# Linear-attention output: r times the state from zero-padded 64-row halves of the array, instead of block-diagonal copies on 128 rows

## The chip, the cores and the metric

The kernel runs on one core of a Trainium2 chip. The metric is device time in microseconds (us) of one execution, start to end; the median of several runs is compared. TensorE (PE in the profile) multiplies, VectorE (DVE) and ScalarE (ACT) work elementwise, GpSimd (POOL) does little here, SyncE (SP) issues the transfers.

## What is computed

The first half is a recurrent linear attention (RWKV-5) for 4 batches, 8 heads, 768 steps and a head width of 48; the second half is a feed-forward network over all 3072 tokens.

```python
state = zeros(B, H, D, D)
for t in range(S):
    cur = (u * k_t)  outer  v_t                 # per head
    y[:, :, t] = r_t @ (state + cur)            # per head, D x D
    state = w[:, :, None] * state + k_t outer v_t
x = y as (3072 tokens, 8 * 48 = 384 features)
out = ((x @ w1) * (x @ w2) @ w3) @ w_out         # 384 -> 1024 -> 1024 -> 384
```

## The kernel before

**Units.** The time steps are cut into 6 chunks `c` of 128 steps, and each chunk is taken for the 4 batches `b` in turn: 24 units `n`. A chunk is two halves `a` of 64 steps. Heads are held in pairs: array `X[rows(i), p]` has head `2p+i` on 64 partitions, `i` = 0 (even) or 1 (odd), of which 48 are used.

**Steps of a unit.** `scale` multiplies k and r by powers of w (L310). `diagonal` makes the u-term (L319 to L321) and eight diagonal blocks of the table `AT` (L326, ScalarE). `turn`, or in later units `turn_blocks`, `turn_places` and `turn_rows`, transposes k and r to features on partitions (L342, or L352, L362 and L367). `pairs` multiplies k with v for the change of the state (L389) and k with r for the table (L395), updates the state twice, once for each half (L403, L408, L409, VectorE), and merges the table into `AT` (L416, VectorE). `output` makes y transposed, features on partitions: r times the state (L473), then the table times v (L483) accumulated onto it, and copies the sum to `xT` (L488, ScalarE).

**The state on the array.** The state `st[b]` holds pair `p` as 48 columns for 128 partitions, even head above, odd head below. L473 multiplies all 128 rows at once, so its stationary operand must be block-diagonal: `spread` (L420, ScalarE) copies the two heads of each pair into different columns of `wide`, whose other columns stay zero. It does so once for the state at the chunk's start (`spread(0, n)`, not in chunk 0) and once for the state after the first half (`spread(1, n)`), two instructions each time, 44 calls and 88 instructions in all. L473 then takes 32 of the 96 columns of a pair at a time: a tile of 128 rows and 32 columns of the array, twelve matmuls for each half. L483, L389 and L395 use tiles of 64 rows and 64 columns; the feed-forward matmuls and the transposes use the whole array.

**PSUM.** `ps_y` is one tile of two banks, one bank for each half `a`, with one buffer. The two banks of `psF` serve all feed-forward products in turn: L500 (x times w1), copied out by ScalarE (L502); L505 (x times w2), multiplied with that copy by VectorE (L506).

**Order.** The feed-forward work on chunk `c-1` and the preparation of its weights stand beside the units of chunk `c` (the lists `beside`): conversion of the weights from 64 to 32 bits (L266 to L272, ScalarE and VectorE), w3 folded with w_out (L296 to L301), then the products `o` (L539 to L553). The engines' queues are in order; a scheduler of the framework decides the order in which each engine's instructions stand, and a few of them are interleaved. In the trace a 32-bit matmul is two pairs of instructions, a weight load (PEld) and a matmul (PE).

Of the kernel before, what the change touches and what calls it, by code (L numbers as in the profile page):

```python
# [8 lines left out]
F32 = mybir.dt.float32  # L9
# [12 lines left out]
def kernel(  # L22
# [10 lines left out]
    moe_w_out: bass.AP,  # L33
    out: bass.AP,
):

# [18 lines left out]
    nc = tc.nc  # L57
    B, H, S, D = r.shape
    P = 128
    C = 128  # L60
    T = C // 2
    HT = T // 2
    NCH = S // C
    PAD = 64
    NP = H // 2
    DM = H * D
    DF = moe_w3.shape[0]
    KM = DM // P
# [7 lines left out]
    Q = 32  # L76
    PD = 2 * D

    const = ctx.enter_context(tc.tile_pool(name="const", bufs=1))

    def rows(i):
        return slice(i * PAD, (i + 1) * PAD)
# [21 lines left out]
    raws = [const.tile([P, RAW], U64, name=f"raw{i}") for i in range(NRAW)]  # L104


    st = [const.tile([P, NP, D], F32, name=f"st{b}") for b in range(B)]
    wide = [[const.tile([P, NP, PD], F32, name=f"wide{a}{i}") for i in range(2)] for a in range(2)]
    two = const.tile([P, 1], F32)
    nc.vector.memset(two, 2.0)  # L110
    wucol = const.tile([P, NP, 1], F32)
# [5 lines left out]
        nc.gpsimd.memset(t[:, :, D:PD], 0.0)  # L117
    for t in krs:
        nc.gpsimd.memset(t[:, :, :, D:PAD], 0.0)
    for t in wide[1] + wide[0]:  # L120
        nc.gpsimd.memset(t, 0.0)
    for t in tts:
        nc.gpsimd.memset(t[:, :, :NP], 0.0)

# [1 line left out]
    units = [(c, b) for c in range(NCH) for b in range(B)]  # L126
# [35 lines left out]
    for i in range(2):  # L162
# [4 lines left out]
                      in_=u.rearrange("h d -> (h d)").rearrange("(o n) -> o n", o=1).to_broadcast([P, DM]))  # L167
# [15 lines left out]
    with tc.tile_pool(name="once", bufs=1) as once, tc.tile_pool(name="psW", bufs=2, space=PSUM) as psW:  # L183
# [12 lines left out]
        for l in range(LEVELS):  # L196
            n = 1 << l
# [6 lines left out]
        for g in range(2):  # L204
            nc.vector.tensor_copy(out=both[:, g, :, T:], in_=both[:, g, :, :T])
            ps = psW.tile([P, NP, C], F32, tag="w", name=f"ps_p{g}")
# [11 lines left out]
    def body(arm, fast):  # L218
# [7 lines left out]
        psY = arm.enter_context(tc.tile_pool(name="psY", bufs=1, space=PSUM))  # L226
# [5 lines left out]
        else:  # L232
# [6 lines left out]
            for l in range(LEVELS):  # L239
                n = 1 << l  # L240
                by = wn[:, l].to_broadcast([P, NP, n])
# [6 lines left out]
            ps = psT.tile([P, NP, C], F32, tag="t", name="ps_pr")  # L248
# [55 lines left out]
        kT, rT, AT, xT = {}, {}, {}, {}  # L304
# [65 lines left out]
        def pairs(n):  # L370

            c, b = units[n]
            kk = krs[n % NS][:, 0]
            if fast:
                au = psA.tile([C, 2, 512], F32, tag="a", name=f"ps_a{n}")
                ps = au[:, :, :NP * T].rearrange("s i (p t) -> s i p t", p=NP)
            else:
                for l in range(LEVELS):
                    level(n, l)
                kk = work.tile([C, H, PAD], F32, tag="rl", bufs=1, name=f"kk{n}")  # L380
                nc.gpsimd.tensor_mul(kk, krs[n % NS][:, 0], pn[:, 0])
                au = psA.tile([C, 2, 512], F32, tag="a", name=f"ps_u{n}")

            up = au[:, :, NP * T:NP * (T + D)].rearrange("x a (p e) -> x a p e", p=NP)
            last = c == NCH - 1
            for p in range(NP):
                for i in range(2):
                    for a in range(1 if last else 2):
                        nc.tensor.matmul(up[rows(i), a, p, :], lhsT=kk[rows(a), 2 * p + i, :],  # L389
                                         rhs=vnat[n % NV][rows(a), 2 * p + i, 0:D], start=True, stop=True)  # L390
            if fast:
                for p in range(NP):
                    for a in range(2):
                        for i in range(2):
                            nc.tensor.matmul(ps[rows(a), i, p, :], lhsT=kT[n][rows(i), p, rows(a)],  # L395
                                             rhs=rT[n][rows(i), p, 2 * a:2 * a + 2], start=True, stop=True)
            by = wc.to_broadcast([P, NP, D])
            if c:
                spread(0, n)
            for a in range(1 if last else 2):  # L400
                if not c and not a:
                    if fast:
                        nc.vector.tensor_mul(st[b], up[:, a], by)  # L403
                    else:
                        nc.vector.tensor_copy(out=st[b], in_=up[:, a])
                elif fast:

                    nc.vector.tensor_add(st[b], up[:, a], st[b])  # L408
                    nc.vector.tensor_mul(st[b], st[b], by)  # L409
                else:  # L410
                    nc.vector.tensor_mul(st[b], st[b], by)
                    nc.vector.tensor_add(st[b], up[:, a], st[b])
                if not a:
                    spread(1, n)
            if fast:
                nc.vector.copy_predicated(AT[n], later.bitcast(I32)[:, None, None, :].to_broadcast([C, 2, NP, T]), ps)  # L416

        def spread(a, n):
            for i in range(2):
                nc.scalar.copy(out=wide[a][n % 2][rows(i), :, i * D:(i + 1) * D], in_=st[units[n][1]][rows(i)])  # L420

        def level(n, l):
            L = 1 << l
# [31 lines left out]
        def output(n):  # L455
            c, b = units[n]
            rw = rT[n]
            if not fast:
                rw = work.tile([P, NP, C], F32, tag="kl", bufs=1, name=f"rw{n}")
                for p in range(NP):  # L460
                    nc.gpsimd.tensor_mul(rw[:, p].rearrange("x (a t) -> x a t", a=2),
                                         rT[n][:, p].rearrange("x (a t) -> x a t", a=2),
                                         pw[:, p, None, :].to_broadcast([P, 2, T]))
            yt = psY.tile([P, 2, 512], F32, tag="y", name=f"ps_y{n}")
            ps = yt[:, :, :KM * T].rearrange("x a (q t) -> x a q t", q=KM)


            blocks = [(p, j, divmod(3 * p + j, P // Q)) for p in range(NP) for j in range(3)]
            to = lambda a, q, g: ps[g * Q:(g + 1) * Q, a, q, :]
            held = range(0 if c else 1, 2)  # L470
            for a in held:
                for p, j, (q, g) in blocks:
                    nc.tensor.matmul(to(a, q, g), lhsT=wide[a][n % 2][:, p, j * Q:(j + 1) * Q], rhs=rw[:, p, 2 * a:2 * a + 2] if fast else rw[:, p, rows(a)],  # L473
                                     start=(q == 0), stop=False, skip_group_check=True)

            vv = vnat[n % NV].rearrange("t h d -> t (h d)")
            parts = [(h, f) for h in range(H) for f in range(h * D // PAD, ((h + 1) * D - 1) // PAD + 1)]
            seen = set()
            for h, f in sorted(parts, key=lambda e: (e[0] * D > e[1] * PAD, e[1])):
                x = h * PD + f * PAD - h * D  # L480
                q, g = divmod(f, 2)
                for a in range(2):
                    nc.tensor.matmul(ps[rows(g), a, q, :], lhsT=vv[rows(a), x:x + PAD], rhs=AT[n][rows(a), h % 2, h // 2, :],  # L483
                                     start=(a not in held and (a, g) not in seen), stop=True, skip_group_check=True)
                    seen.add((a, g))
            if b == 0:
                xT[c] = work.tile([P, KM, NT], F32, tag="xT", bufs=2, name=f"xT{c}")
            nc.scalar.copy(out=xT[c][:, :, b * C:(b + 1) * C].rearrange("x q (a t) -> x a q t", a=2), in_=ps)  # L488


        abt, lead = {}, 3 if fast else 1
# [110 lines left out]
        diagonal(0)  # L602
        turn(0)
        pairs(0)
        asked = 2
        for c in range(NCH):
# [4 lines left out]
            for b in range(B):  # L611
                n = c * B + b
                while asked <= (n + 3 if n + 3 >= free else n + 2):
                    load(asked, "kr")
                    asked += 1
                load(n + 2, "v")
                if n + 1 < min(NU, free):
                    scale(n + 1)
                if n + 1 < NU:
                    diagonal(n + 1)  # L620
                    if n + 1 >= free:
                        turn_rows(n + 1)
                if n + 1 < min(NU, free):
                    turn(n + 1)
                if free <= n + 2 < NU:
                    scale(n + 2)
                    turn_blocks(n + 2)
                for step in plan[2 * b]:
                    step()
                output(n)  # L630
                if free <= n + 2 < NU:
                    turn_places(n + 2)
                if n + 1 < NU:
                    pairs(n + 1)
                for step in plan[2 * b + 1]:
                    step()
# [41 lines left out]
```

## Time and profile before

| what | value |
|---|---|
| median of 6 runs | 526.64 us (525.91 to 528.13) |
| the profiled execution | 526.08 us, of which the profile's span is 524.1 us |
| PE busy | 496.1 us, 95% of the span |
| PE weight loads busy | 324.8 us, 62% |
| DVE busy | 281.4 us, 54% |
| ACT busy | 195.4 us, 37% |
| L473, r times the state | 1056 matmul instructions, 25.2 us busy |
| L483, the table times v | 1152 matmul instructions, 24.4 us busy |
| L420, copies of the state | 88 instructions, 30.7 us of ACT |
| L488, y out of PSUM | 24 instructions, 11.4 us of ACT |

A row of a group gives the time in which any of its instructions ran and the mean time of one; matmuls overlap, so the sum of the single times is much larger than the busy time. The share of an engine is a mean over stages: up to about 50 us VectorE and ScalarE are the busy ones, after that PE is busy almost throughout.

### The profile page before, as it was taken

How to read it: one execution, taken by the hardware profiler on the slowest of the kernel's cores; microseconds unless marked ns; L12 is line 12 of the kernel's file. 1: busy time of each engine (PE TensorE's matmuls, PEld its weight loads, DVE VectorE, ACT ScalarE, POOL GpSimd, SP SyncE). 2: the span in 40 equal slices, each digit the busy share in tenths (PEclk: the TensorE clock that was granted, in tenths of full speed). 3: DMA queues.
4: the chain of work that ended last, by engine and by line, in shares of the span. 5: the costliest groups of instructions: out<-in, count | busy, mean ns of one | idle time of the engine just before them, and what ended most of it. 6: DMA issues, size and time to landing. Idle time of an engine off the chain costs nothing.

```text
span 524.1 us, 12272 instructions
## 1 busy us (share of the span) xinstructions
PE 496.1 (95%) x5192; PEld 324.8 (62%) x5192; DVE 281.4 (54%) x616; ACT 195.4 (37%) x487; POOL 6.0 (1%) x23
## 2 busy tenths in 40 slices
PE   2797999999999999999999999999999999999996
PEld 2586555455555656649646965498555777954486
DVE  5899887579765566492633374334431216211442
ACT  3897475557654666330223124212143110001000
POOL 4000000000000000000000000000000000000000
PEclk9887999999999999999999999999999999999999
DMA  7988665758685463230131324111120000000001
GB/s 186 237 220 240 178 152 139 197 150 202 169 260 128 161 187 108 44 102 31 48 90 39 99 70 99 45 52 55 35 77 28 1 32 31 32 30 1 0 6 61
DMA packets 96866, 52.73 MB, mean 101 GB/s; under 512 B 77729, under 2 KB 88226, under 8 KB 96802
## 3 DMA queue, kind: packets, MB, share of 16 engines
q1 hardware_dynamic: 96802, 51.86, 36.6%
q8 instruction: 43, 0.70, 0.6%
q14 instruction: 21, 0.17, 0.1%
HBM read 39.65 MB, written 12.19 MB: 99 GB/s over the span
## 4 chain that ended last, share of the span: by engine, by line
PE 82%; DVE 7%; ACT 5%; DMA 3%; issue 1%; SPq 0%; DVEq 0%; ACTq 0%
PE ps_b L505 22%; PE ps_a L500 22%; PE ps_w L300 7%; PE ps_s3t L539 3%; PE ps_s4b L539 3%; PE ps_s1t L539 3%; PE ps_a22t L539 3%; PE ps_y L483 3%; PE ps_y L473 3%; PE ps_a12b L539 3%; PE ps_s2t L539 3%; PE ps_a11b L539 3%; ACT AT L326 2%; DMA raw<-in_moe_w_dram 2%; PE ps_a L395 2%
## 5 line engine op out<-in xcount | busy, mean ns | idle before, releaser
L500 PE MATMUL ps_a<-xT,w 128*128 128x512 f32 (+1 forms) x300 | 134.9, 586 | 0.0
L505 PE MATMUL ps_b<-xT,w 128*128 128x512 f32 (+1 forms) x300 | 133.1, 578 | 0.2 <-DVE abt L506 0.2
L505 PEld LDWEIGHTS ps_b<-xT,w 128*128 128x128 f32 x300 | 56.3, 190 | 65.8 <-issue 59.5
L506 DVE TENSOR_TENSOR abt<-ps_b,a 128x512 f32<-128x512 f32 (+1 forms) x50 | 33.4, 668 | 116.9 <-PE ps_b L505 116.8
L500 PEld LDWEIGHTS ps_a<-xT,w 128*128 128x128 f32 x300 | 56.0, 193 | 58.6 <-issue 53.0
L502 ACT COPY a<-ps_a 128x512 f32<-128x512 f32 (+1 forms) x50 | 28.4, 568 | 148.7 <-PE ps_a L500 148.3
L326 ACT ACTIVATE AT<-same,dg 128x64 f32<-128x64 f32 x192 | 48.8, 337 | 0.3
L420 ACT COPY wide<-st 64x192 f32<-64x192 f32 x88 | 30.7, 349 | 43.5 <-PE ps_y L473 27.5
L300 PE MATMUL ps_w<-wo,w3T 128*128 128x384 f32 x128 | 43.1, 490 | 2.4 <-ACT w3T L297 2.4
L300 PEld LDWEIGHTS ps_w<-wo,w3T 128*128 128x128 f32 x128 | 23.7, 190 | 17.9 <-ACT w3T L297 2.9
L473 PEld LDWEIGHTS ps_y<-tt,wide 128*32 128x32 f32 x1056 | 18.3, 111 | 24.0 <-issue 15.7
L310 DVE TENSOR_TENSOR krs<-krin,pn_in 128x768 f32<-128x768 f32 x24 | 22.9, 954 | 18.9 <-PE ps_a L389 9.4
L473 PE MATMUL ps_y<-tt,wide 128*32 128x64 f32 x1056 | 25.2, 226 | 6.7 <-ACT wide L420 3.9
L271 ACT ACTIVATE t<-raw,two 128x512 f32<-128x512 uint32 (+2 forms) x32 | 25.5, 802 | 10.7 <-DVE wo L269 5.5
L266 ACT ACTIVATE power<-raw 128x512 f32<-128x512 f32 (+2 forms) x32 | 22.4, 706 | 12.0 <-DMA raw<-in_moe_w_dram 10.9
L483 PE MATMUL ps_y<-AT,vnat 64*64 64x64 f32 x1152 | 24.4, 233 | 1.8 <-DVE AT L416 1.8
L483 PEld LDWEIGHTS ps_y<-AT,vnat 64*64 64x64 f32 x1152 | 20.8, 145 | 6.6 <-DVE AT L416 2.2
L545 ACT COPY m<-ps_a11b 128x192 f32<-128x192 f32 x12 | 3.8, 318 | 53.5 <-PE ps_a11b L539 53.5
L267 DVE TENSOR_SCALAR power<-power 128x512 f32<-128x512 f32 (+2 forms) x32 | 14.0, 437 | 11.0 <-ACT power L266 10.8
L488 ACT COPY xT<-ps_y 128x384 f32<-128x384 f32 x24 | 11.4, 473 | 21.5 <-PE ps_y L483 15.6
L395 PE MATMUL ps_a<-tt,kT 64*64 64x64 f32 x768 | 18.3, 230 | 0.7 <-issue 0.7
L352 DVE STREAM_TRANSPOSE tr<-krs 128x768 f32<-128x768 f32 x19 | 18.5, 975 | 0.5
(92 smaller groups left out, 582.0 us busy)
## 6 DMA issues: line engine op xcount, KB each, us to landing
raw<-in_moe_w_dram SPq DMA_DIRECT2D x16, 512.0 KB, 4.9
scratch<-tr SPq DMA_DIRECT2D x19, 384.0 KB, 3.3
raw<-in_moe_w_dram SPq DMA_DIRECT2D x8, 768.0 KB, 6.1
tt<-scratch SPq DMA_DIRECT2D x38, 128.0 KB, 2.8
krin<-in_k_dram SPq DMA_DIRECT2D x24, 192.0 KB, 4.0
krin<-in_r_dram SPq DMA_DIRECT2D x24, 192.0 KB, 4.2
vnat<-in_v_dram SPq DMA_DIRECT2D x24, 192.0 KB, 3.7
out_dram<-osb SPq DMA_DIRECT2D x24, 192.0 KB, 1.9
```

The source lines that it names most:

```text
L271: nc.scalar.activation(out=t, in_=lo, func=IDENTITY, bias=two, scale=2.0 ** -51)
L300: nc.tensor.matmul(ps, lhsT=w3T[:, kc, :], rhs=wo[kc], start=(kc == 0), stop=(kc == KF - 1))
L326: nc.scalar.activation(out=AT[n][:, i, p, :], in_=same, func=COPY, scale=dg[:, h:h + 1])
L395: nc.tensor.matmul(ps[rows(a), i, p, :], lhsT=kT[n][rows(i), p, rows(a)], rhs=rT[n][rows(i), p, 2 * a:2 * a + 2], start=True, stop=True)
L420: nc.scalar.copy(out=wide[a][n % 2][rows(i), :, i * D:(i + 1) * D], in_=st[units[n][1]][rows(i)])
L473: nc.tensor.matmul(to(a, q, g), lhsT=wide[a][n % 2][:, p, j * Q:(j + 1) * Q], rhs=rw[:, p, 2 * a:2 * a + 2] if fast else rw[:, p, rows(a)] ...
L483: nc.tensor.matmul(ps[rows(g), a, q, :], lhsT=vv[rows(a), x:x + PAD], rhs=AT[n][rows(a), h % 2, h // 2, :], start=(a not in held and (a, g ...
L500: nc.tensor.matmul(pa[:, :n], lhsT=w1[:, z, q, js], rhs=xT[c][:, q, ts], start=(q == 0), stop=(q == KM - 1))
L502: nc.scalar.copy(out=a[:, :n], in_=pa[:, :n])
L505: nc.tensor.matmul(pb[:, :n], lhsT=w2[:, z, q, js], rhs=xT[c][:, q, ts], start=(q == 0), stop=(q == KM - 1))
L506: nc.vector.tensor_mul(abt[c, j][:, ts], pb[:, :n], a[:, :n])
L539: nc.tensor.matmul(ps, lhsT=made[c, j][a][:, m * C:(m + 1) * C], rhs=made[b][:, j, :], start=(j == 0), stop=(j == KH - 1))
```

## The change

The state is kept in one array `st` whose layout already has zeros between the pairs of heads: 48 zeros, 48 state columns, 48 zeros, and so on. It has B + 1 = 5 places for the states at a chunk's start, taken in rotation, and one for the state after a first half, which all units share. VectorE writes each new state straight into its next place, so `wide` and `spread` are gone. r times the state is now made on 64 rows and 64 columns: even heads come from the upper 64 partitions and go to PSUM tile `y0`, odd heads from the lower 64 to `y1`; a block of 64 features that reaches over a head's end reads the zeros beside it. The number of these matmuls stays at twelve for each half, in an order that takes the four 64x64 quarters of the array in turn. The table times v adds its first half to `y0` and its second half to `y1`. ScalarE copies `y0` to `xT`; VectorE then adds `y1` to it, for both halves, or for the second half alone in chunk 0.

```diff
-    st = [const.tile([P, NP, D], F32, name=f"st{b}") for b in range(B)]
-    wide = [[const.tile([P, NP, PD], F32, name=f"wide{a}{i}") for i in range(2)] for a in range(2)]
+    st = const.tile([P, D + (B + 2) * NP * PD], F32)
...
             by = wc.to_broadcast([P, NP, D])
-            if c:
-                spread(0, n)
             for a in range(1 if last else 2):
+                new = features(state(n + B, 0) if a else state(n, 1))
+                old = features(state(n, a))
                 if not c and not a:
                     if fast:
-                        nc.vector.tensor_mul(st[b], up[:, a], by)
+                        nc.vector.tensor_mul(new, up[:, a], by)
...
                 elif fast:
-                    nc.vector.tensor_add(st[b], up[:, a], st[b])
-                    nc.vector.tensor_mul(st[b], st[b], by)
+                    nc.vector.tensor_add(new, up[:, a], old)
+                    nc.vector.tensor_mul(new, new, by)
...
-                if not a:
-                    spread(1, n)
...
-        def spread(a, n):
-            for i in range(2):
-                nc.scalar.copy(out=wide[a][n % 2][rows(i), :, i * D:(i + 1) * D], in_=st[units[n][1]][rows(i)])
+        def state(n, a):
+            x = (B + 1 if a else n % (B + 1)) * NP * PD
+            return st[:, x:x + D + NP * PD]
+
+        def features(t):
+            return t[:, D:].rearrange("x (p e) -> x p e", e=PD)[:, :, :D]
...
-            yt = psY.tile([P, 2, 512], F32, tag="y", name=f"ps_y{n}")
-            ps = yt[:, :, :KM * T].rearrange("x a (q t) -> x a q t", q=KM)
-            blocks = [(p, j, divmod(3 * p + j, P // Q)) for p in range(NP) for j in range(3)]
...
-                for p, j, (q, g) in blocks:
-                    nc.tensor.matmul(to(a, q, g), lhsT=wide[a][n % 2][:, p, j * Q:(j + 1) * Q], rhs=rw[:, p, 2 * a:2 * a + 2] if fast else rw[:, p, rows(a)],
-                                     start=(q == 0), stop=False, skip_group_check=True)
+            yt = [psY.tile([P, 2, KM, T], F32, tag=f"y{i}", name=f"ps_y{n}_{i}") for i in range(2)]
...
+            quarters = [[e for e in parts if (e[0] % 2, e[1] % 2) == z] for z in ((0, 0), (1, 1), (0, 1), (1, 0))]
+            for a in range(0 if c else 1, 2):
+                for h, f in [e for four in zip(*quarters) for e in four]:
+                    p, i = divmod(h, 2)
+                    x = D + p * PD + f * PAD - h * D
+                    nc.tensor.matmul(**to(i, a, f), lhsT=state(n, a)[rows(i), x:x + PAD],
+                                     rhs=rw[rows(i), p, 2 * a:2 * a + 2] if fast else rw[rows(i), p, rows(a)])
...
-                    nc.tensor.matmul(ps[rows(g), a, q, :], lhsT=vv[rows(a), x:x + PAD], rhs=AT[n][rows(a), h % 2, h // 2, :],
+                    nc.tensor.matmul(**to(a, a, f), lhsT=vv[rows(a), x:x + PAD], rhs=AT[n][rows(a), h % 2, h // 2, :])
...
-            nc.scalar.copy(out=xT[c][:, :, b * C:(b + 1) * C].rearrange("x q (a t) -> x a q t", a=2), in_=ps)
+            x = xT[c][:, :, b * C:(b + 1) * C].rearrange("x q (a t) -> x a q t", a=2)
+            nc.scalar.copy(out=x, in_=yt[0])
+            held = slice(0 if c else 1, 2)
+            nc.vector.tensor_add(x[:, held], yt[1][:, held], x[:, held])
```

The helper `to(i, a, f)` gives the place of feature block `f` of half `a` in tile `y<i>`, and starts a new sum at the first write to each half of the partitions of each tile.

## The prediction

> **What bounds the kernel now.** I read the page first, then the windows, the list of waits and single stretches of the timeline. First the page's engine shares, then windows of 10 us (PE, PEld, DVE, ACT, POOL busy, then granted clock, DMA share, GB/s):
>
> ```profile
> PE 496.1 (95%) x5192; PEld 324.8 (62%) x5192; DVE 281.4 (54%) x616; ACT 195.4 (37%) x487; POOL 6.0 (1%) x23
> ```
>
> ```profile
> 20.00:30.00 10.00, 7.55 (x193) 6.25 (x197) 9.75 (x19) 9.85 (x28) 0.00 (x0) 0.68 0.94 240
> 40.00:50.00 10.00, 6.21 (x147) 5.31 (x146) 10.00 (x19) 8.13 (x23) 0.00 (x0) 0.71 0.87 251
> 70.00:80.00 10.00, 9.01 (x151) 4.71 (x151) 9.18 (x19) 7.10 (x21) 0.00 (x0) 1.00 0.70 160
> 220.00:230.00 10.00, 10.00 (x157) 5.61 (x156) 9.07 (x20) 5.23 (x15) 0.00 (x0) 1.00 0.25 61
> ```
>
> Until 50 us VectorE and ScalarE are full and PE waits; from there on PE is full but for short waits. So the change is worth what it takes off PE's own stream after 50 us, plus the waits it ends, minus those it makes. ScalarE time by itself is worth nothing after 50 us.
>
> The timeline of one unit in a quiet stretch (start, length in us, engine, line) shows PE's stream around the change:
>
> ```profile
> 376.76 0.19 PEld L505 LDWEIGHTS ps_b<-xT,w 128*128 128x128 f32 x1 [0.24 <-issue]
> 377.71 0.72 PEld L473 LDWEIGHTS ps_y<-tt,wide 128*32 128x32 f32 x48 [0.76 <-issue]
> ...
> 378.52 0.79 PEld L483 LDWEIGHTS ps_y<-AT,vnat 64*64 64x64 f32 x48
> ...
> 379.22 0.50 PEld L389 LDWEIGHTS ps_a<-vnat,krs 64*64 64x64 f32 x14
> ...
> 379.67 0.57 PEld L395 LDWEIGHTS ps_a<-tt,kT 64*64 64x64 f32 x30
> ```
>
> With the median length of one load (110 ns in L473, 135 ns in L483, by the lists of the two lines) the starts can be worked out. L473: (0.72 - 0.11) / 47 = 13.0 ns from start to start. L483: (0.79 - 0.135) / 47 = 13.9 ns. From L473's last start (378.32) to L483's first: 0.20 us. From L483's last (379.17) to L389's first: 0.04 us, and there the tile shape stays. Changing from 128x32 to 64x64 tiles thus costs 0.16 us on top of a step.
>
> The other rows that the sum uses are the groups (count, busy us, mean ns, idle before and its cause) and the waits of PE for `wide`:
>
> ```profile
> L420 ACT COPY wide<-st 64x192 f32<-64x192 f32 x88 | 30.7, 349 | 43.5 <-PE ps_y L473 27.5 <-DVE st L409 14.0 <-DVE st L403 1.0
> L546 DVE TENSOR_TENSOR osb<-ps_a12b,m 128x192 f32<-128x192 f32 x12 | 4.3, 357 | 21.0 <-PE ps_a12b L539 20.4 <-issue 0.6
> L506 DVE TENSOR_TENSOR abt<-ps_b,a 128x512 f32<-128x512 f32 x46 | 31.7, 690 | 116.6 <-PE ps_b L505 116.5
> ```
>
> ```profile
> PE ps_y L473 <- ACT wide L420: 3.9, 3, 2.4
> PE ps_y L483 <- DVE AT L416: 1.8, 2, 1.3
> ```
>
> **PE's stream after 50 us.** The built orders of PE tell how often tile shapes change. Before, a 128x32 and a 64x64 burst meet 23 times (L473 to L483 21 times, L395 to L473 twice); afterwards never, as r times the state then has the shape of its neighbours. Three of these lie in chunk 0, where PE waits anyway: 20 x 0.16 = -3.2 us. Entries from the full array into a small tile and back remain, 34 against 35 after chunk 0; an entry costs 377.71 - 376.76 = 0.95 instead of the usual 0.43, an exit less, so one entry and exit fewer is about -0.4.
>
> Against this, each load has 64 columns instead of 32. The number of matmuls is the same, 960 instructions after chunk 0. The nearest rows for their step are L483 (13.9, same quarters in turn, same moving length) and L395 ((0.57 - 0.13) / 29 = 15 ns, same moving operand); the far end is L389 in the last chunk, where only two of the four quarters are used: (0.50 - 0.135) / 13 = 28 ns. A gain in the step is excluded, since no burst of 64-column loads steps under 13.7. I take L483's, as order and quarters match: 960 x 1.0 to 1.1 ns = +1.1 us, with +2 us for L395's and +14 us for L389's. [...] The rows do show the longer load (135 against 110 ns), but the starts move by only 1 ns, since loads into different quarters overlap; so the sum goes by the steps. PE's stream: -3.2 - 0.4 + 1.1 = **-2.5 us**.
>
> **Copies of the state.** 88 x 0.349 = 30.7 us of ScalarE go. After 50 us they stood on PE's path in three places. At 73.05 PE idles 0.92 us for `wide`: both copies (0.73) and two hops go, but the new add of the unit before now stands ahead of the state's update in VectorE's order (+0.5), so I take -0.4. At 139.02 PE idles 1.03 us for w3T, which stands in ScalarE's queue behind AT, xT, two conversions and, at 134.06, two copies of 0.72 together: -0.6 (what is late next is the conversion's VectorE part). At 198.6 the chain has two copies again (0.6), ahead of a weight transfer that is waited for: -0.4. Sum **-1.4 us**, between 0 and -2.
>
> **The added VectorE work.** Four adds of 128x192 from PSUM, 0.357 each as in L546, and twenty of 128x384, not in the trace: above 0.357, below the 0.690 of 128x512 in L506, by the line between them 0.56. Together 12.6 us. Each waits for ScalarE's copy of `y0` (0.47), and queued behind it on VectorE stand krs (L310), the block transpose (L352), the state updates (L408) and the merge (L416) of the next unit, for which PE's next `output` waits, and sometimes an abt product (L506), which frees a bank for PE. After 240 us VectorE is at half load and less, and a unit's `output` follows 10 us or more later: nothing. Between 80 and 220 us PE's slack covers about 1 us a unit: nothing, if the cover holds; the rival prices it. From 220.9 to 236 us VectorE is the late one: sums of weights, sums of abt, one unit. There PE waited 0.20 and 0.51 us for L506. One add comes in (0.5 at the spacing of neighbours) and PE arrives 0.16 us sooner: **+0.6 us**.
>
> **The first 50 us.** The last long wait of PE there ends at 45.41, when VectorE has merged AT of unit 3 (the 1.3 in the list above). VectorE has hardly a gap from 17.5 us to then, so what stands ahead in its order counts. In the built order of the changed kernel one join of converted weights (0.91 at its spacing), one clamp (0.47) and two ruk products (0.47 each) move behind that merge, and three adds (0.3 each at their spacing) come in: -2.3 + 0.9 = -1.4. Some of it is lost where an add or abt product now waits at the head (up to 0.7 us at the first L506, as PE isn't faster by as much). What moved behind is next needed by L505 after PE's 5 us of products that follow. The two hops over ScalarE in chunk 0 (2.4 us of wait at 43.17) mostly turn into wait for the merge. I take **-0.8 us**, from -2 to +1.5 (four adds in full, nothing gained).
>
> **Sum.** -2.5 - 1.4 + 0.6 - 0.8 = -4.1 us. Of the profiled execution's 526.08 us (span 524.1 and 2 around it) that leaves 522.0. The median of the runs was 0.56 us above the profiled one, so the time to expect is 526.64 - 4.1 = 522.5 us. With the terms' own bounds taken together this case reaches from 520 to 525. A difference under 0.3% (1.6 us) can't be told from none.
>
> **Rivals.** *VectorE's queue becomes the path.* Place: units 4 to 12, 66 to 236 us, where VectorE still converts weights. If PE's slack there is under the 1.1 us of copy, hop and add (0.47 + 0.1 + 0.56), nine units pay it: +9.9 - 2.5 - 0.8 = +6.6, about 533 us. For it speaks DVE at 9.2 and 9.1 of 10 at 70 and 220 us; against it, that PE waited for the state at one unit of these nine only. Chance 0.08.
> *The quarters don't overlap*, so the change doesn't do on the array what it says: 28 ns as in L389's short burst, +14 us instead of +1.1: 536 us. L483 speaks against it with the same turn of quarters. Chance 0.04.
> *It evens out.* Step of 15 ns (+2), no wait ended, the start +1 and the stretch at 230 us +0.8: -3.6 + 2 + 1 + 0.8, about 526.8 us. Chance 0.11.
> *The start gains more*: -2 there, all of -2 from copies, and the clock, 0.68 and 0.71 in two windows above, comes up sooner (0.5 to 1 us): 518 us. Chance 0.06.
>
> **How the numbers follow.** The main case has 0.71. Faster: 0.71 + 0.06 = 0.77; same: 0.11; slower: 0.08 + 0.04 = 0.12. The range 519 to 527.5 takes in the main case and the even one, and leaves out about 0.18.
>
> **What would show it.** Right: the new matmuls start 14 ns apart, with 0.04 us to the table's burst behind them; no wait of PE for ScalarE at that line; the adds near 0.56 us; AT of unit 3 merged before 45 us; PE's wait near 236 us up by half a microsecond. Wrong: PE or its loads waiting for `st` or AT in units 4 to 12 by more than before, a step over 16 ns, or L506 ending waits of PE between 80 and 220 us.

## The result, and the profile after

The changed kernel takes 529.24 us (median of 29 runs, 525.85 to 534.96), against 526.03 us for the kernel before in the runs beside it (66 runs, 523.97 to 529.05): ratio 1.0063, 95% interval 1.0049 to 1.0076. It is 3.3 us slower where 4.1 us faster was forecast. Two of its executions, 534.79 and 534.96 us, lie over 1.5% above its fastest and are left out of the ratio. Ratios and intervals are worked out from the single runs, so a ratio need not be the quotient of the medians shown. The profiled execution took 528.0 us (span 526.2).

The page's shares, then the same windows of 10 us as shown of before (PE, PEld, DVE, ACT, POOL busy, granted clock, DMA share, GB/s):

```profile
PE 494.2 (94%) x5192; PEld 325.6 (62%) x5192; DVE 292.0 (55%) x640; ACT 163.8 (31%) x399; POOL 6.6 (1%) x20
```

```profile
20.00:30.00 10.00, 8.09 (x272) 6.92 (x264) 9.86 (x20) 8.91 (x24) 0.00 (x0) 0.71 0.95 222
40.00:50.00 10.00, 6.93 (x144) 6.14 (x145) 9.20 (x19) 6.22 (x21) 0.00 (x0) 0.66 0.94 254
70.00:80.00 10.00, 10.00 (x164) 5.45 (x157) 9.32 (x20) 5.47 (x16) 0.00 (x0) 0.83 0.46 112
220.00:230.00 10.00, 10.00 (x165) 5.96 (x164) 6.77 (x15) 4.08 (x12) 0.00 (x0) 1.00 0.25 61
```

PE is busy 1.9 us less, ScalarE 32 us less, VectorE 11 us more. But at 70 to 80 us PE, though full, has a clock of 0.83, where before it had 1.00.

The timeline of the same quiet unit (start, length, engine, line) shows PE's stream as forecast:

```profile
379.35 0.19 PEld L515 LDWEIGHTS ps_b<-xT,w 128*128 128x128 f32 x1 [0.24 <-issue]
380.30 0.79 PEld L485 LDWEIGHTS ps_y<-tt,st 64*64 64x64 f32 x48 [0.76 <-issue]
380.99 0.80 PEld L492 LDWEIGHTS ps_y<-AT,vnat 64*64 64x64 f32 x48
381.69 0.50 PEld L388 LDWEIGHTS ps_a<-vnat,krs 64*64 64x64 f32 x14
...
382.15 0.57 PEld L394 LDWEIGHTS ps_a<-tt,kT 64*64 64x64 f32 x30
```

L485, r times the state, steps by (0.79 - 0.135) / 47 = 13.9 ns; its last start is 380.955 and L492 begins 0.035 us later, where it was 0.20. From the last full load to the final L394 burst it takes 2.80 us, before 2.91: 0.11 us a unit, as worked out.

The groups of VectorE (form, count, busy us, mean ns, idle before) and the waits of PE (total, times, longest):

```profile
L498 DVE TENSOR_TENSOR xT<-ps_y,xT 128x384 f32<-128x384 f32 x20 | 11.1, 555 | 15.1 <-ACT xT L496 11.1 <-PE ps_a L394 4.0
L498 DVE TENSOR_TENSOR xT<-ps_y,xT 128x192 f32<-128x192 f32 x4 | 1.4, 345 | 0.0
```

```profile
PE ps_y L485 <- DVE st L402: 4.6, 2, 2.5
...
PE ps_a L510 <- DVE xT L498: 1.9, 1, 1.9
...
PE ps_b L515 <- DVE abt L516: 1.6, 2, 0.8
...
PE ps_y L485 <- ACT xT L496: 1.5, 1, 1.5
```

The adds have the forecast length. Nobody waits for `wide` any more; the waits now go to `st`, xT and abt. The two for `st` and the one of L510 for xT lie before 50 us.

**Where the time goes in the trace.** I put landmarks (the end of each unit's L492 burst against that of L483 before) side by side. The changed kernel is 1.7 us ahead at 66 us, 0.3 behind at 76, 2.6 behind at 135, 2.7 behind at 260, and then gains 0.11 a unit to 2.2 behind. So the start gave more than forecast, the quiet stretch what was forecast, and 66 to 135 us took over 4 us. The timeline shows the largest piece:

```profile
66.19 0.96 DVE L268 SCALAR_TENSOR_TENSOR w<-power,t 128x768 uint32<-128x768 uint32 x1
...
67.19 1.00 ACT L270 ACTIVATE t<-raw,two 128x768 f32<-128x768 uint32 x1 [1.61 <-DVE w L268]
...
68.09 0.46 ACT L496 COPY xT<-ps_y 128x384 f32<-128x384 f32 x1
68.22 0.96 DVE L271 CUSTOM_DVE_ANT_0 w<-w,t 128x1536 uint16<-128x1536 uint16 x1
...
68.61 0.44 PE L485 MATMUL ps_y<-tt,st 64*64 64x64 f32 x6 [1.49 <-ACT xT L496]
69.10 0.55 DVE L498 TENSOR_TENSOR xT<-ps_y,xT 128x384 f32<-128x384 f32 x1
...
69.70 0.56 PE L485 MATMUL ps_y<-tt,st 64*64 64x64 f32 x18 [0.65 <-DVE xT L498]
```

The table's product was done at 65.97. ScalarE's copy of it stands behind a conversion step (L270) that waits for VectorE's L268; the copy begins at 68.09. Then the add stands behind a conversion step too (L271), and PE waits again, for the second bank. In before the conversion and the copy behind it run at the same times, though PE gets there 1.5 us later and so waits for only 0.17 us:

```profile
67.28 1.03 ACT L271 ACTIVATE t<-raw,two 128x768 f32<-128x768 uint32 x1
...
68.20 0.47 ACT L488 COPY xT<-ps_y 128x384 f32<-128x384 f32 x1
...
68.81 0.54 PE L473 MATMUL ps_y<-tt,wide 128*32 128x64 f32 x24 [0.17 <-ACT xT L488]
```

So PE's lead buys nothing at this place, as the copy is no earlier; and with the second wait, the feed-forward products behind begin at 70.19 us, where they began at 69.29. Right behind it the clock falls, in windows of 2.5 us:

```profile
67.50:70.00 2.50, 0.74 (x22) 0.60 (x24) 2.47 (x6) 2.50 (x9) 0.00 (x0) 1.00 0.43 105
70.00:72.50 2.50, 2.50 (x29) 0.93 (x25) 2.50 (x5) 1.95 (x5) 0.00 (x0) 0.53 0.20 40
72.50:75.00 2.50, 2.50 (x28) 1.31 (x21) 2.50 (x7) 0.00 (x0) 0.00 (x0) 0.79 0.89 236
```

2.5 x (0.47 + 0.21) = 1.7 us lost in this execution: a stretch of 3.4 us at half clock (granted clock 0.50 from 70.2 to 73.5 us). Further new waits of PE are 0.78 us at 118 (L515 for L516), 0.85 at 124 (issue), and 0.53 at 178, where w34's copy (L300) on ScalarE stands behind a conversion's first step that waited for a transfer of weights until 177.61:

```profile
177.61 0.66 ACT L265 ACTIVATE power<-raw 128x512 f32<-128x512 f32 x1 [2.78 <-DMA raw<-in_moe_w_dram]
178.17 0.46 ACT L300 COPY w<-ps_w 128x384 f32<-128x384 f32 x1
```

### The profile page after: what moved, and what is told of

It is laid out like the page before. It is cut to its first block, busy times and chain, and to the rows that moved or that the text cites. A ratio compares the mean times of both kernels' runs of the same rounds, so it can differ in the third digit from the quotient of the medians.

```text
span 526.2 us, 12230 instructions
## 1 busy us (share of the span) xinstructions
PE 494.2 (94%) x5192; PEld 325.6 (62%) x5192; DVE 292.0 (55%) x640; ACT 163.8 (31%) x399; POOL 6.6 (1%) x20
## 4 chain that ended last, share of the span: by engine, by line
PE 78%; DVE 10%; ACT 4%; DMA 4%; SPq 2%; issue 2%; DVEq 0%; ACTq 0%
PE ps_a L510 21%; PE ps_b L515 20%; PE ps_w L299 7%; PE ps_y L485 3%; PE ps_s3t L549 3%; PE ps_s4b L549 3%; PE ps_s1t L549 3%; PE ps_a22t L549 3%; PE ps_a12b L549 3%; PE ps_s2t L549 3%; PE ps_y L492 3%; PE ps_a11b L549 3%; DMA raw<-in_moe_w_dram 2%; DMA krin<-in_r_dram 2%; PE ps_a L394 2%
## 5 line engine op out<-in xcount | busy, mean ns | idle before, releaser
L510 PE MATMUL ps_a<-xT,w 128*128 128x512 f32 (+1 forms) x300 | 136.7, 591 | 1.9 <-DVE xT L498 1.9
L515 PE MATMUL ps_b<-xT,w 128*128 128x512 f32 (+1 forms) x300 | 132.4, 577 | 1.6 <-DVE abt L516 1.6
L515 PEld LDWEIGHTS ps_b<-xT,w 128*128 128x128 f32 x300 | 56.8, 191 | 68.2 <-issue 60.0
L516 DVE TENSOR_TENSOR abt<-ps_b,a 128x512 f32<-128x512 f32 (+1 forms) x50 | 33.4, 668 | 113.4 <-PE ps_b L515 113.2
L510 PEld LDWEIGHTS ps_a<-xT,w 128*128 128x128 f32 x300 | 56.3, 194 | 59.6 <-issue 53.1
L485 PEld LDWEIGHTS ps_y<-tt,st 64*64 64x64 f32 x1056 | 20.7, 138 | 25.8 <-issue 12.3
L485 PE MATMUL ps_y<-tt,st 64*64 64x64 f32 x1056 | 26.4, 229 | 7.4 <-DVE st L402 4.6
L270 ACT ACTIVATE t<-raw,two 128x512 f32<-128x512 uint32 (+2 forms) x32 | 25.3, 800 | 21.4 <-DVE wo L268 10.1
L492 PE MATMUL ps_y<-AT,vnat 64*64 64x64 f32 x1152 | 23.0, 227 | 1.4 <-DVE AT L413 1.4
L492 PEld LDWEIGHTS ps_y<-AT,vnat 64*64 64x64 f32 x1152 | 20.6, 142 | 3.6 <-DVE AT L413 2.5
L394 PE MATMUL ps_a<-tt,kT 64*64 64x64 f32 x768 | 19.5, 232 | 1.5 <-issue 1.5
L498 DVE TENSOR_TENSOR xT<-ps_y,xT 128x384 f32<-128x384 f32 (+1 forms) x24 | 12.5, 520 | 15.1 <-ACT xT L496 11.1
```

Source lines behind the costliest of these rows:

```text
L270: nc.scalar.activation(out=t, in_=lo, func=IDENTITY, bias=two, scale=2.0 ** -51)
L485: nc.tensor.matmul(**to(i, a, f), lhsT=state(n, a)[rows(i), x:x + PAD], rhs=rw[rows(i), p, 2 * a:2 * a + 2] if fast else rw[rows(i), p, ro ...
L492: nc.tensor.matmul(**to(a, a, f), lhsT=vv[rows(a), x:x + PAD], rhs=AT[n][rows(a), h % 2, h // 2, :])
L510: nc.tensor.matmul(pa[:, :n], lhsT=w1[:, z, q, js], rhs=xT[c][:, q, ts], start=(q == 0), stop=(q == KM - 1))
L515: nc.tensor.matmul(pb[:, :n], lhsT=w2[:, z, q, js], rhs=xT[c][:, q, ts], start=(q == 0), stop=(q == KM - 1))
L516: nc.vector.tensor_mul(abt[c, j][:, ts], pb[:, :n], a[:, :n])
```

## The experiments

In each set of runs the kernel before ran beside. Ratios are to it, with 95% intervals; "lag" is the landmark's time minus that of before in the profiled runs. The build orders the engines' steps anew for every kernel: by the traces, of the 616 VectorE steps that before and after share, at least 91 stand in another order (and 25 of 399 on ScalarE); in the first two experiments it is 34 and 40, and in after without the add, set against after, 39. So no experiment here changes the load of an engine and nothing else.

### First set: the add's time, its bank, or its engine

**Before with an operation of the add's size, and the same without the second bank's hold.** The second reads xT twice in the place of the bank.

```
-            nc.scalar.copy(out=xT[c][:, :, b * C:(b + 1) * C]..., in_=ps)
+            x = xT[c][:, :, b * C:(b + 1) * C].rearrange("x q (a t) -> x a q t", a=2)
+            nc.scalar.copy(out=x, in_=ps)
+            held = slice(0 if c else 1, 2)
+            nc.vector.tensor_tensor(x[:, held], ps[:, held], x[:, held], ALU.max)
```

> The kernel before, with one VectorE instruction more in each unit at the place of the new add: the maximum of ps_y and xT after ScalarE's copy (the two are equal, so the values stay); state copies, array tiles and banks as before. Theory A (the serial second step of emptying ps_y, on VectorE's queue while it is full, is what cost the gain): 3 to 6 us slower than before, about 530 us, with PE waiting for VectorE between 60 and 240 us. Rival B (the new tiles, the state's layout or the changed order of the other work cost it, not the step): within 1 us of before, 525 to 527 us.

Measured: 530.55 us, ratio 1.0067 (1.0045 to 1.0089).

> As the run with the maximum, but the VectorE instruction reads xT twice and not ps_y, so the banks come free with ScalarE's copy while VectorE's time and queue are the same. Theory A splits in two: if the held bank is what costs, this is within 1 us of before (526); if VectorE's time and the wait at the head of its queue cost, it is as slow as the run with ps_y, about 529 to 530 us. Rival B: 525 to 527 us.

Measured: 530.06 us, 1.0065 (1.0043 to 1.0087). That the bank is held longer makes no difference that shows. The work on VectorE, with the order that the build gives its steps around it and nothing else of the change, costs 3.5 us (uncertain by 1.1), and not the 0.6 of the forecast. PE's waits between 60 and 320 us in the first of the two show most of where (before: 0.5 us for a12b, 0.2 for L505, 0.2 for xT, and 0.9 for `wide`, which nobody waits for here):

```profile
PE ps_y L473 <- DVE xT L491: 1.9, 2, 1.7
...
PE ps_a12b L542 <- DVE abt L509: 1.2, 1, 1.2
PE ps_b L508 <- DVE abt L509: 1.0, 2, 0.7
```

**After without the add.**

```
-            nc.vector.tensor_add(x[:, held], yt[1][:, held], x[:, held])
```

> The changed kernel without VectorE's add: the odd heads' share of r times the state and the second half's table times v are left out of xT, all else is there. Theory A: the gain forecast for PE's stream and the copies appears, 3 to 5 us faster than before, 521 to 523 us. Rival B: no faster than before, 526 to 529 us.

Measured: 528.45 us, 1.0020 (0.9994 to 1.0046). Against after that is 1.0063 / 1.0020: the add costs about 2.2 us, uncertain by 1.5. But the forecast without its add was 4.7 us faster, and this is 1.1 slower (from 0.3 faster to 2.4 slower). So about 5.8 us are missing that are not the add's. Its profile again has three waits close together where VectorE and ScalarE are late in units 4 and 5 (PE's waits, 64 to 80 us), and then half clock from 74.9 to 78.3 us (granted clock 0.99, 0.50 and 0.83 in the windows of 2.5 us from 72.5 us on):

```profile
PE ps_y L485 <- DVE st L408: 1.0, 1, 1.0
PE ps_y L492 <- DVE AT L413: 0.8, 1, 0.8
PE ps_y L485 <- ACT xT L496: 0.7, 1, 0.7
```

**After with the add on GpSimd** (from chunk 1 on; ScalarE copies `y1` to the dead table first, as GpSimd reads it there).

```
-            nc.vector.tensor_add(x[:, held], yt[1][:, held], x[:, held])
+            nc.scalar.copy(out=odd, in_=yt[1])
+            nc.gpsimd.tensor_add(x, odd, x)
```

> The changed kernel, but after chunk 0 ScalarE copies y1 too, into the unit's dead table AT, and GpSimd adds it to xT, so VectorE has four adds instead of 24. Theory A: most of the gain comes back, 1 to 4 us faster than before, 522 to 525 us, unless the longer way to xT makes PE wait at the start of a chunk. Rival B: as slow as the changed kernel or slower, 528 to 531 us.

Measured: 541.23 us, 1.0273 (1.0250 to 1.0296). The second copy and a GpSimd add of 1.33 us lengthen every chain; PE waits 7.0 us in three places for ScalarE's copies of w3T between 130 and 240 us alone.

### Second set: VectorE relieved, and the copies alone

**Before without the copies of the state** from the third chunk on.

```
         def spread(a, n):
+            if n >= 2 * B:
+                return
```

> Before, with ScalarE's copies of the state left out from the third chunk on (TensorE then multiplies r with a state that is not brought up to date; the wait for the copies is gone, all else stays). It prices the removed copies alone. The prediction's term: the copies' removal gives 1.4 us, so a ratio of about 0.9975 for these (some less than that, since the copies of the first two chunks stay: only the waits near 139 and 198 us go, 1.0 us). The theory that the waits named after the copies are only the last of several late inputs: PE waits as long for VectorE's st or AT instead, and the ratio is 0.999 to 1.001.

Measured: 525.97 us, 0.9982 (0.9963 to 1.0001). In the trace the lag stays between 0.0 and 0.4 us from 31 us on, and PE's waits at 138.1 (1.02 us) and 207.9 (0.66) are within 0.05 us of those of before. The term for these two places (1.0 of its 1.4 us) is not seen there: the wait ends with something else at the same time. The ratio alone doesn't decide it, as its interval holds both a gain of 1.0 us (0.9981) and none. The third place, at 73.05 us, lies before the third chunk and isn't tested by this.

**The two products of the diagonal on GpSimd,** in before, in after, and in after without the add.

```
-            nc.vector.tensor_mul(ruk, kr[:, 0], kr[:, 1])
-            nc.vector.tensor_mul(ruk, ruk, ub)
+            nc.gpsimd.tensor_mul(ruk, kr[:, 0], kr[:, 1])
+            nc.gpsimd.tensor_mul(ruk, ruk, ub)
```

> Before, with the two products for the diagonal (k times r, times u; 2 x 0.55 us a unit on VectorE, 24 units, 26 us in all) made by GpSimd, which is idle there. Theory V (between 60 and 135 us VectorE's queue sets when TensorE gets its inputs, so every us put on or taken from that queue moves the end): faster, by 1 to 3 us, ratio 0.994 to 0.998. Theory C (the forecast gain is not in TensorE's stream at all, or is lost to TensorE's clock after clusters of waits): 0.999 to 1.001. Against both: GpSimd's 2 x 1.3 us a unit come late for AT and hold up the merge, or slow VectorE: over 1.002.

Measured: 537.71 us, 1.0195 (1.0173 to 1.0216).

> After, with the same two products on GpSimd: VectorE loses 26 us of work against the 12.5 us that the adds put on it. Theory V: the loss of 3.3 us goes and the forecast gain appears, ratio to before 0.988 to 0.995, and it is faster than the same edit of before by 2 to 4 us. Theory C: the distance to the edit of before stays +3 us, ratio about 1.006.

Measured: 533.84 us, 1.0125 (1.0102 to 1.0149).

> After without VectorE's add (odd heads' share of r times the state, and the second half's table times v, are left out of xT), with the two products on GpSimd. Theory V: once VectorE has room its adds cost little, so within 1 us of the same kernel with the adds. Theory that the adds cost by the chain from TensorE over ScalarE and VectorE to the next user, whatever else VectorE has to do: 2 us or more faster than with the adds.

Measured: 534.11 us, 1.0136 (1.0113 to 1.0160). All are slower than before (GpSimd's pair takes 2.3 us where VectorE's took 1.1), but after with this edit is 3.9 us **faster** than before with it: the forecast's size, but not its places. Up to 122 us the two edited kernels' lags lie within 2 us of each other, 0.6 apart at the last landmark there. By the next, the edited before loses 3.6 us, with one wait of PE of 2.09 us at 134.66 (for ScalarE's copy of `a`) and a half-clock stretch from 136.9 to 140.3 us (granted clock 0.88, 0.50 and 0.93 in the windows of 2.5 us from 135 us on); the edited after loses 1.2. So 2.4 of the 4.1 us by which their profiles end apart come from one place. The add makes no difference there that shows.

### Third set: the same relief in other ways

**Products on GpSimd in units 5 to 12 only, half a unit early** (written into the table's own tile).

```
+                if fast and 5 <= n + 2 <= 12:
+                    products(n + 2, nc.gpsimd)
```

> Before, with the two products for the diagonal on GpSimd in units 5 to 12 only, and half a unit earlier than before (into the table's own tile, so that no room is needed). What the earlier GpSimd kernels lost in the first 50 us, where the products came late, should not be lost here. Theory V (VectorE's queue sets the pace at 60 to 135 us): 0 to 2 us faster than before, ratio 0.996 to 1.000. If GpSimd slows VectorE's other work by as much as it takes from it: 1.000 to 1.004.

Measured: 541.27 us, 1.0291 (1.0267 to 1.0315).

> After, with the same edit. Theory V: 3 to 4 us faster than the same edit of before, as in the pair with all units on GpSimd, ratio to before 0.988 to 0.994: faster than both kernels. If that pair's 3.9 us came from the first 50 us alone: no faster than the same edit of before.

Measured: 542.54 us, 1.0289 (1.0268 to 1.0310). Theory V missed in both kernels; after is no faster than the same edit of before, as the second text's other case has it, though the traces don't bear out its reason: in the pair with all units on GpSimd, after leads by only 0.9 us at 47 us. The timeline of the edited before shows the price: the diagonal's sum stands at the head of VectorE's queue for 1.97 us, waiting for GpSimd, with everything else behind it.

```profile
79.73 1.34 POOL L318 TENSOR_TENSOR AT<-krin 128x384 f32<-128x384 f32 x1 [7.23 <-ACT t L271]
...
81.15 0.99 POOL L319 TENSOR_TENSOR AT<-AT,ub 128x384 f32<-128x384 f32 x1
...
82.18 0.55 DVE L328 TENSOR_REDUCE dg<-AT 128x8 f32<-128x384 f32 x1 [1.97 <-POOL AT L319]
```

**Products left out,** in units 4 to 12, and in all (the sum runs over k alone).

```
-            nc.vector.tensor_mul(ruk, kr[:, 0], kr[:, 1])
-            nc.vector.tensor_mul(ruk, ruk, ub)
-            nc.vector.tensor_reduce(dg, ruk, AX.X, ALU.add)
+            nc.vector.tensor_reduce(dg, kr[:, 0], AX.X, ALU.add)
```

> Before, with the two products for the diagonal left out in units 4 to 12 (the sum then runs over k alone, so those diagonals are other values): 9 x 1.1 = 9.9 us less on VectorE between 45 and 135 us, and nothing put on GpSimd. Theory V: a little faster, since before waits little there (1.7 us of PE's idle gaps over 0.15 us between 50 and 130 us): 0 to 2 us, ratio 0.996 to 1.000.

Measured: 525.54 us, 0.9974 (0.9957 to 0.9990).

> After, with the same left out: 9.9 us less on VectorE, where nine units' adds put on 4.7 us. Theory V: the loss turns into the forecast gain, 3 to 4 us faster than the same edit of before, ratio to before 0.988 to 0.994. Theory that the loss is not VectorE's queue (the order of the units' steps, or TensorE's clock after waits): it stays 2 to 3 us slower than the same edit of before, ratio 1.003 to 1.006.

Measured: 526.98 us, 1.0004 (0.9988 to 1.0020).

> Before, with the two products for the diagonal left out in all 24 units (the diagonals are other values): 26 us less on VectorE, 11 us of them in the full first 60 us. Theory V (VectorE's queue sets the pace up to 135 us): 2 to 5 us faster than before, ratio 0.990 to 0.996.

Measured: 526.30 us, 0.9998 (0.9978 to 1.0019).

> After, with the same left out. Theory V: with room on VectorE everywhere the forecast gain appears, 3 to 4 us faster than the same edit of before, as in the pair with the products on GpSimd. Theory O (the build puts VectorE's steps, above all the product that frees a bank of TensorE's, in another order, and that order costs 2 to 3 us whatever the load): it stays 1 to 2 us slower than the same edit of before.

Measured: 528.25 us, 1.0022 (1.0000 to 1.0045). 10 or 26 us less on VectorE bring the distance of after to before from +0.63% to +0.30 and +0.24% (each uncertain by 0.2 to 0.3), not to the forecast's -0.8. Theory V alone falls. Theory O's 1 to 2 us for the last pair fit (1.3), and the rival of the pair before it (2 to 3 us, the order or the clock) fits within the uncertainty (1.6). In after without products PE still waits in units 4 and 5 (0.72 us for ScalarE's xT, 0.77 for the add, 0.62 for AT), and 0.76 at 176 us behind w34's copy.

### Fourth set: other levers on after

**The state's multiplication on ScalarE** in units 4 to 12.

```
-                    nc.vector.tensor_mul(new, new, by)
+                    for p in range(NP):
+                        nc.scalar.activation(out=new[:, p], in_=new[:, p], func=COPY, scale=wc[:, p])
```

> After, with the state's multiplication by its factor in units 4 to 12 made by ScalarE (four instructions in the place of one of VectorE's 0.34 us): VectorE gives up 16 x 0.34 = 5.4 us, about what the nine adds of this stretch put on it, and ScalarE takes back part of what the removed copies left free. Theory V: 1 to 2 us faster than after, ratio to before 1.002 to 1.004. If ScalarE's queue is as tight, or the state comes too late for TensorE: 1.006 or more.

Measured: 531.80 us, 1.0101 (1.0069 to 1.0133): slower, in line with a ScalarE queue that is as tight; a wait of 1.78 us for its copy of `a` appears at 116 us.

**xT's copy, the add and the abt product put first in the build's order.**

```
+            with tc.high_priority(offset=100):
                 nc.vector.tensor_mul(abt[c, j][:, ts], pb[:, :n], a[:, :n])
```

> After, with ScalarE's copy of xT, VectorE's add and VectorE's product that ends a pair of 128x128 multiplications put ahead of other ready steps in the build's order (the product then stands ahead of the last multiplication of the state in the units with such a product, 0.34 us earlier). Theory O: the waits for the product at 118 and 233 us shrink, 0.3 to 1 us faster than after. Theory V: no change, since what stands ahead of it has to be done anyway.

Measured: 529.62 us, 1.0060 (1.0037 to 1.0082): no change. The waits at 119 and 234 us stay at 0.79 and 0.78: moving the product past one step of 0.34 us isn't enough. By the trace the edit moved 4 of VectorE's 640 steps and none of ScalarE's, so xT's copy still stood behind the conversion at 68 us, and PE waited 1.86 us for it: the copy's place was not tested.

### Fifth set: does a lead reach the end?

**Before with 1.9 us less for PE,** at 60 us or at 105 us.

```
-            for q in range(KM):
+            KA = KM - 1 if (c, j) == (0, 3) else KM
+            for q in range(KA):
```

> Before, with a third of one 128x512 pair of products left out (the last of three blocks of the sum, in both, of the pair that ends at 66 us): TensorE has 1.9 us less to do ahead of unit 5's r times the state. It asks alone whether a lead that TensorE gains before 66 us reaches the end. The prediction's way of counting (what comes off TensorE's stream comes off the time): 1.9 us faster, ratio 0.9964. Theory L (the copy of xT and the state of units 4 and 5 stand in ScalarE's and VectorE's queues behind conversion steps whose times the weights' transfers set, so TensorE waits there until the same time as before): 0 to 0.6 us faster, ratio 0.999 to 1.000.

Measured: 524.66 us, 0.9972 (0.9961 to 0.9983): 1.5 of the 1.9 us reach the end. That doesn't refute theory L: in this kernel ScalarE makes xT's copy ahead of the conversion step (L271) behind which it stood in before, the only kernel here with this order, and the wait that theory L counts on isn't there (the later one for `wide` is 1.31 us, in before 0.92).

```profile
66.08 0.48 ACT L488 COPY xT<-ps_y 128x384 f32<-128x384 f32 x1
...
68.37 0.99 ACT L271 ACTIVATE t<-raw,two 128x768 f32<-128x768 uint32 x1
```

What it shows is that a lead at 66 us can reach the end where the copy follows PE at once.

> Before, with the same third left out of a pair of chunk 1's products near 105 us. The prediction's way of counting: 1.9 us faster, ratio 0.9964. Theory L, where it holds for the whole stretch in which weights come in (to 220 us, with waits for converted weights at 137 and 138 us): under 1 us faster, ratio over 0.998.

Here (1, 1) stands for (0, 3). Measured: 528.18 us, 1.0043 (1.0026 to 1.0060): with **less** work, 2.3 us slower. In both kernels PE's order is nearly that of before, but the build moved other steps: by the traces at least 19 (first) and 27 (second) of VectorE's 616, and 7 and 11 of ScalarE's 487. The lag is +0.6 us at 135 and +3.2 at 163. The waits of PE between 125 and 145 us, and the windows behind them:

```profile
PE ps_w3T L296 <- DVE w3n L272: 2.2, 2, 1.3
```

```profile
140.00:142.50 2.50, 2.44 (x7) 1.64 (x8) 2.50 (x7) 2.46 (x7) 0.00 (x0) 0.58 0.54 108
142.50:145.00 2.50, 2.50 (x7) 1.42 (x6) 2.47 (x6) 1.15 (x3) 0.00 (x0) 0.74 0.44 161
```

The conversion of w3n, waited for by 0.22 us before, comes later in VectorE's order; PE waits 0.89 and 1.30 us for it, and then loses 2.5 x (0.42 + 0.26) = 1.7 us to a half-clock stretch. (Before also waits 1.03 us for w3T at 138; this one doesn't.)

## Why the prediction was wrong, point by point

**What held.** PE's stream: step, transitions and the gain of 0.11 us a unit are in the trace as forecast. The adds' length (555 and 345 ns for a forecast 560 and 357). The start: at 66 us five profiles of the changed stream (after, its two edits without products, and the two of the fourth set) lie 1.4 us ahead of before on average, and five of the old stream (before, without copies, the two without products, and the one with less work at 105 us) 0.7 behind, so about 2 us for the forecast 0.8 (by like pairs: 1.7, 1.8 and 2.1). AT of unit 3 is merged at 43.6 us, before 45 as forecast. The wait near 236 us: 0.78 + 0.51 against 0.20 + 0.51, up by 0.6 as forecast; without the add it is 0.66 + 0.18, so about 0.45 of the 0.6 go with the add.

**The step that failed** is "*The added VectorE work*", where the text says: "Between 80 and 220 us PE's slack covers about 1 us a unit: nothing, if the cover holds". It didn't hold. Put into before, the same work costs 3.5 us (forecast 0.6), and in after it costs about 2.2, in both with the steps' order changed around it. The rival named the right place and mechanism (66 to 236 us, VectorE's queue), at nine units paying 1.1 us each; what happens is a few waits of 0.5 to 1.7 us where an xT or abt stands behind a conversion step. The largest lie at 67 to 71 us, just ahead of the stretch that the text names, where the sum charged the add with nothing but 0.5 at `wide`. The sign that would show it wrong, L506's like ending waits of PE between 80 and 220 us, is there at 118; and the sign for being right, no wait of PE for ScalarE at the new line, fails with the 1.49 us at 67.

**The second failure is the sum itself.** Its terms were priced one by one against before's own order of steps and added. Without the add, -4.7 was due and about +1.1 came. What it got wrong, by after's profile from 66 us on: PE's lead was taken to stay, but at 67 us xT's copy, behind a conversion, came at the same time as in before; the wait for `wide` at 73.05 was taken as shortened by 0.4; with the copies gone, PE's wait in units 4 and 5 was for xT, and was 2.14 us in all, 1.05 more than the two waits of before there (0.17 and 0.92); with it came, in this execution, 1.7 us of half clock; 0.78 + 0.85 + 0.53 us of new waits at 118, 124 and 178. Of the term for the copies, the wait at 139.02 (1.03) is 0.69 in after, half of the 0.6 forecast, and the 0.4 of 198.6 is not seen. Two slips on the way changed nothing: the terms of the rival that has the start gain more add up to about 520 us, not 518, and one burst of 64-column loads in before, at 30.6 us, steps by 13.5 ns, under the 13.7 that the text gives as the least.

**How much rests on the surroundings** the same change shows against five versions of them (the two ratios to before divided, with their half intervals added in squares):

| surroundings | after / before |
|---|---|
| as they are | 1.0063 ± 0.0014 |
| products left out in units 4 to 12 | 1.0030 ± 0.0023 |
| products left out in all units | 1.0024 ± 0.0030 |
| products on GpSimd, units 5 to 12, early | 0.9998 ± 0.0032 |
| products on GpSimd, all units | 0.9931 ± 0.0032 |

PE's own gain is in the trace of each of the changed kernels: their lag falls by about 0.1 us a unit over the last six units, while that of the old stream stays. What else happens around it moves the result by 7 us from end to end, part of it by single events such as the 3.6 us that the edited before loses at 134 us in the last row. The last experiment shows the size of this by itself: less work in another order, 2.3 us slower.

**The clock** spreads the runs but isn't the cause of the mean. Over the 31 executions with records, those of after at a mean clock of 0.977 to 0.981 had spans of 531.5 to 533.2 us, those at 0.993 to 0.995 had 524.2 to 526.0 on average at each clock. A half-clock stretch costs 1.7 / 526 = 0.0032 of mean clock, and by the line through the 31 points (417 us for each unit of clock; 353 without the two longest) 1.1 to 1.4 us of span. But the mean clock of after's runs is 0.9874, that of before's 0.9870. These are means over whole executions; where the half clock fell is known for the profiled ones alone.

**Open:** how the missing 5.8 us divide between the new order of steps and the fuller queues. No kernel with the new stream in the old order was run, and none of the changed ones has xT's copy ahead of the conversion at 67 us. No version here with the full computation beats the kernel before.

## What to carry to other kernels

Where an in-order queue serves both conversions and the copies that the bound engine waits for, price an edit by the queue at each place, not by busy shares: 0.5 us more a unit cost 3.5 us, while 9.9 us less in nine units gave 1.4 and 26 us less in all units gave nothing. A saving of under 1% on the bound engine can be smaller than what a build's new order of steps takes; compare the built orders on all engines first, look for copies that slip behind steps that wait for transfers, and leave room for it in the range. Removing what a wait is named after ends the wait only if nothing else arrives at the same time. And before an experiment is read as one on load alone, compare its built order too: here each one moved other steps.

## What the runs showed of the hardware

In some of these profiles PE's granted clock fell to 0.50 for 3.4 us after waits that are short each. In after 1.49 and 0.65 us within 2.6 us (0.44 us of small products between them) were followed by such a stretch, from 70.1 to 73.6 us, and in before with less work at 105 us 0.89 and 1.30 within 3.3 us; in before waits of 0.17 and 0.92 were not, nor 1.31 alone in before with less work at 60 us. No sharp bound shows: after without products in all units had 0.72, 0.77 and 0.62 us within 6 us and kept full clock (1.00 in every window of 2.5 us from 65 to 80 us); a single wait of 2.09 us (before, products on GpSimd in all units, 134.66 us) was followed by half clock, and one of 2.62 us (after with the raised priority, 50.53 us) was not (1.00 in the windows from 50 to 70 us). What decides between these cases was not shown.

GpSimd took 1.10 to 1.22 us on average for a product of 128x384 (1.15 and 1.12 in before with the products on GpSimd in all units, 1.15 and 1.22 in after with them, 1.13 and 1.10 in the eight early units of after), for which VectorE took 0.55 in before, and 1.33 us for the add (after with the add on GpSimd), for which VectorE took 0.555 in after. In before with the products on GpSimd in all units some of VectorE's steps took longer on average than in before: the state's factor (L409) 404 ns instead of 341, the conversion step L272 on `w` 1154 instead of 947; others did not, as L408 with 344 and 339 ns or L416 with 722 and 719.
